# A planned attention and mixture-of-experts kernel: turns for VectorE and GpSimd, due times by product, another product order at group ends, an earlier warm-up

## The chip, the cores and the metric

The kernel runs on one core of a Trainium2 chip. The metric is device time in microseconds (us) of one execution. A kernel's time is the median of its runs; the profile shows one execution with its own time. TensorE multiplies matrices and does the transposes, VectorE and GpSimd do element-wise work, ScalarE does exponentials, casts and copies, and SyncE issues the DMA loads and stores. A profile calls them PE (PEld is its weight load), DVE, POOL, ACT and SP.

## The reference

Windowed attention feeds a dense mixture of four experts.

```python
scores = scale * np.matmul(q, k.transpose(0, 1, 3, 2))      # q, k, v: (4, 8, 576, 64)
rel = pos[:, None] - pos[None, :]
mask = (rel >= 0) & (rel < 64)
scores = np.where(mask, scores, -1e9)
attn = np.exp(scores - np.max(scores, axis=-1, keepdims=True))
attn = attn / (np.sum(attn, axis=-1, keepdims=True) + 1e-09)
x = np.matmul(attn, v).transpose(0, 2, 1, 3).reshape(2304, 512)
p = domain_probs / (domain_probs.sum(-1, keepdims=True) + 1e-09)
for e in range(4):
    h = np.maximum(x @ w1[e], 0.0)                           # w1[e]: (512, 1024)
    out += p[:, e:e + 1] * (h @ w2[e])                       # w2[e]: (1024, 512)
```

## The kernel before, in words

**The work.** The 2304 rows of x are three groups of 768. A group is made by 12 attention steps of 64 rows, numbered g = 0 to 35. Step g has scores on TensorE (`S`, tile `sb`), row maxima on VectorE (`st`), exponentials on ScalarE (`sm`), reciprocals on VectorE, the normalisation on GpSimd (`sm` again, line 356), a transpose on TensorE (`tb`), its copy (`pt`), the product with v on TensorE (`vb`) and a copy into the group's x^T tile `xr`.

For each group the four experts are 16 units of 256 hidden columns, 48 units in all. The units are numbered 0 to 47; units 16 and 32 are the first of the second and third group, units 15 and 31 the last before. Each matrix is split into a high part (a cast to fp32r) and a low part (the value minus the high part), and a product is three fp32r multiplications: high by high, high by low, low by high.

**First layer.** Units 0 and 1 multiply directly (tile `d`). All others use Strassen's scheme in Winograd's form: seven products P1 to P7 instead of eight, of the four quarters of x^T (B11, B12, B21, B22) and combinations of them (T1 to T4, made in `xr` itself by three-operand subtractions, line 426), with combinations of the raw weights `w1r` (sums on GpSimd, lines 468 to 471). A product is six matmuls of 384 columns. P1 goes to the PSUM bank X, P5 to V, P6 to Y; P7 and P4 add to Y, P2 adds to X, P3 to V. ScalarE copies P1's result to `s1`, and P2 may write X only after that. VectorE forms `u2`, `u3`, `c22`, `c21`, `c12` from the banks (line 595). The relu is split in turn: high part on ScalarE (line 535), low part on VectorE (line 538), both into tiles `h`.

**Second layer.** For a pair of units and each of six row tiles, two half steps of six matmuls (tile `y`, 128x512) multiply `h` with `w2s`. VectorE adds each finished `y`, scaled by p, to the accumulator `acc` (line 676). The low part of `w2s` is made on GpSimd (line 510), two instructions of 512 columns.

**The order.** The list `seq` fixes TensorE's order of products and second-layer halves. Everything else is a `Step` with a cost for each engine that may do it, a due time, the steps it comes after and the buffers it needs. `Planner.order` walks a clock for each engine, takes the ready step that can start first (among equals the one due first), puts it on the engine where it ends first and frees buffers. The steps are then emitted in the planned order, so each engine runs a fixed queue. A unit's halves of the second layer stand between the products of the next units, one after each product from the second on.

The loads stand in SyncE's one queue. Weights are reloaded for each group. `w1r` has two buffers, `w2r` one, `w2s` three, and each split piece of a unit's w1 (`w1a` to `w1d`) one.

**At a group's end.** The last unit of a group still needs the old x^T parts, so the splits of the next group's parts become possible one by one while the last unit's products run. The due times of all of them were counted from one number, `due0`, eight places ahead of the new group's first product.

**At the start.** 20 fp32 matmuls of 128 columns on the identity matrix (`warm`, line 716, 40 instructions) precede the first scores. The weights p are normalised by `prep` (lines 520 to 523, four VectorE instructions).

Of the kernel before, what the change touches and what calls it, by code (L numbers as in the profile page):

```python
# [29 lines left out]
class Step:  # L30
    def __init__(self, plan, name, engines, emit, due, after=(), takes=(), uses=(), seq=None):
        self.name, self.engines, self.emit, self.due, self.seq = name, engines, emit, due, seq
# [11 lines left out]
class Planner:  # L44
# [5 lines left out]
    def order(self):  # L50
# [3 lines left out]
        dma_free = 0.0  # L54
# [12 lines left out]
        while left:  # L67
            best = None
            for e, now in clock.items():
                cands = []  # L70
                for s in ready[e]:
                    if s.seq is not None and s.seq != seq_at:
                        continue
                    t = max(now, s.ready)
# [23 lines left out]
            clock[e] = end  # L98
            if e == "SP":
# [23 lines left out]
def kernel(ctx: ExitStack, tc: tile.TileContext, q, k, v, dprobs, w1, w2, out):  # L123
    nc = tc.nc
# [75 lines left out]
    def dvec(n):  # L200
        return 0.1 + 0.00056 * n

    def pool_(n):
        return 0.1 + 0.00225 * n

    def add(name, engines, emit, due, after=(), takes=(), uses=(), seq=None):
        return Step(plan, name, engines, emit, due, after, takes, uses, seq)
# [8 lines left out]
    FIRST = ("P1", "P2", "P5", "P6", "P7", "P4", "P3")  # L216
# [9 lines left out]
    for i in range(DIRECT, nun + 4):  # L226
# [5 lines left out]
        prods = [("p", i, j) for j in (FIRST if i % NU == 0 or i == DIRECT else ORDER)] if i < nun else []  # L232
# [20 lines left out]
    for g in range(NG):  # L253
# [97 lines left out]
        r = add(f"r{g}", dict(DVE=0.42), recip, due + 1.8, [e], [], [st])  # L351
# [6 lines left out]
        nm = add(f"n{g}", dict(POOL=0.05 + 0.00203 * NP * nk), norm, due + 2, [r], [], [sm, st])  # L358
# [39 lines left out]
    for n in range(NGRP):  # L398
        due0 = at["p", n * NU, "P1"] - 8 if n else at["p", DIRECT, "P1"] - 10
# [6 lines left out]
        def split(name, q_, after, due, n=n, quarter=quarter, src=src):  # L406
            b = comb[n, name] = Buf("T4" if name == "B12" else name)

# [9 lines left out]
            h = add(f"{name}h{n}", dict(ACT=act(KH * T), DVE=dvec(KH * T)), hi, due, after, [b], [src])  # L418
            l = add(f"{name}l{n}", dict(DVE=dve(KH * T), POOL=pool_(KH * T)), lo, due + 0.1, [h], [], [src, b])
# [3 lines left out]
        def diff(name, dst, a, b_, after, due, n=n, quarter=quarter, src=src):  # L423
# [4 lines left out]
            s = add(f"{name}d{n}", dict(DVE=dve(KH * T), POOL=pool_(KH * T)), sub, due, after, [], [src])  # L428
# [3 lines left out]
        b11 = split("B11", 0, x0, due0 if n else -60)  # L432
# [346 lines left out]
```

## Time and profile before

| | us |
|---|---|
| median of 3 runs | 868.26 |
| lowest and highest run | 867.0, 871.38 |
| the profiled execution's own time | 868.09 |
| its span, first to last instruction | 866.3 |
| TensorE busy in the span | 845.9 |
| VectorE busy | 605.0 |
| ScalarE busy | 358.0 |
| GpSimd busy | 330.6 |

TensorE is busy in 98% of the span, VectorE in 70%. The ends of matmuls are modelled in a profile, so durations of neighbours overlap; what a step costs TensorE is read from start to start. Outside the span lie 1.8 us.

### The profile page before, as it was taken

The page shows a single profiled execution, that of the slowest core. Times are in us where ns is not written, and L with a number is a line of the kernel's source. Part 1 is how long each engine was busy: PE and PEld are TensorE (multiplying, and loading weights), DVE is VectorE, ACT ScalarE, POOL GpSimd, SP SyncE. Part 2 cuts the span into 40 slices and gives each one's busy share as a digit, 9 for nine tenths or more (in the row PEclk, how much of TensorE's full clock was granted, in tenths as well). Part 3 has the DMA queues.
Part 4 walks back from the last instruction along what each step waited for, and adds up shares of the span by engine and source line. Part 5 has one row for each costly group of instructions (what it writes and reads, how often), then busy time and mean ns, then how long its engine had stood idle before and what let it go on. Part 6 is the DMA issues. An engine that isn't in the chain of part 4 may idle for free.

```text
span 866.3 us, 12968 instructions
## 1 busy us (share of the span) xinstructions
PE 845.9 (98%) x4816; PEld 755.0 (87%) x4816; DVE 605.0 (70%) x965; ACT 358.0 (41%) x825; POOL 330.6 (38%) x336
## 2 busy tenths in 40 slices
PE   7899999999999989999999999997999999999998
PEld 7788988888888888888888888886988988999896
DVE  3878767667676897666766767697667667667652
ACT  4645434445444455333443544343334334334320
POOL 3464424344244453342434424354243244333301
PEclk9999999999999999999999999998999999999999
DMA  9933313233233142312323212112232112212001
GB/s 308 301 111 104 97 50 97 96 101 104 92 113 114 49 153 98 122 61 74 119 78 120 72 39 84 63 48 86 75 108 73 57 66 73 74 49 97 26 24 73
DMA packets 45327, 81.23 MB, mean 94 GB/s; under 512 B 6352, under 2 KB 15568, under 8 KB 45264
## 3 DMA queue, kind: packets, MB, share of 16 engines
q1 hardware_dynamic: 45264, 80.40, 27.9%
q8 instruction: 38, 0.62, 0.3%
q14 instruction: 25, 0.20, 0.1%
HBM read 75.67 MB, written 4.72 MB: 93 GB/s over the span
## 4 chain that ended last, share of the span: by engine, by line
PE 90%; DVE 6%; DMA 2%; issue 1%; SPq 0%; ACT 0%; ACTq 0%
PE y L657 44%; PE Y L576 16%; PE X L576 11%; PE V L576 11%; PE sb L298 2%; PE vb L378 2%; PE tb L363 1%; PE d L629 1%; DVE T L416 1%; DVE xr L426 1%; DVE B L416 1%; DMA kt<-in_k_dram 1%; DMA vn<-in_v_dram 1%; DMA w1r<-in_moe_w_dram 1%; DVE h L538 0%
## 5 line engine op out<-in xcount | busy, mean ns | idle before, releaser
L657 PE MATMUL y<-w2s,h 128*128 128x512 f32 x1728 | 447.7, 396 | 0.0
L657 PEld LDWEIGHTS y<-w2s,h 128*128 128x128 f32 x1728 | 320.0, 188 | 52.1
L510 POOL TENSOR_TENSOR w2s<-w2r,w2s 128x512 fp32r<-128x512 f32 x96 | 135.8, 1436 | 164.2 <-ACT w2s L506 159.5
L676 DVE SCALAR_TENSOR_TENSOR acc<-y,dp,acc 128x512 f32<-128x512 f32 x126 | 94.1, 747 | 114.7 <-PE y L657 114.5
L468 POOL TENSOR_TENSOR w1r<-w1r 128x256 f32<-128x256 f32 x46 | 36.8, 801 | 229.6 <-DMA w1r<-in_moe_w_dram 206.9
L538 DVE SCALAR_TENSOR_TENSOR h<-c,h 128x384 fp32r<-128x384 f32 x138 | 112.6, 816 | 6.6 <-ACT h L535 6.5
L535 ACT ACTIVATE h<-c 128x384 fp32r<-128x384 f32 x138 | 72.4, 525 | 49.3 <-DVE c L595 45.9
L595 DVE TENSOR_TENSOR u<-Y,s 128x384 f32<-128x384 f32 x92 | 51.1, 555 | 48.6 <-PE Y L576 48.1
L506 ACT CAST w2s<-w2r 128x1024 fp32r<-128x1024 f32 x48 | 50.4, 1050 | 78.1 <-DMA w2r<-in_moe_w_dram 63.7
L356 POOL TENSOR_TENSOR sm<-sm,st 128x512 f32<-128x512 f32 (+1 forms) x36 | 38.8, 1078 | 111.0 <-DVE st L349 102.2
L486 ACT CAST w1b<-w1r 128x512 fp32r<-128x512 f32 x46 | 28.5, 619 | 98.0 <-PE Y L576 96.1
L595 DVE TENSOR_TENSOR c<-V,u 128x384 f32<-128x384 f32 x92 | 51.1, 556 | 24.2 <-PE V L576 22.7
L576 PE MATMUL X<-B,w1c 128*128 128x384 f32 x276 | 58.1, 346 | 7.1 <-ACT s L598 7.1
L576 PEld LDWEIGHTS X<-B,w1c 128*128 128x128 f32 x276 | 50.0, 191 | 11.2 <-ACT s L598 7.6
L486 ACT CAST w1c<-w1r 128x512 fp32r<-128x512 f32 x48 | 29.8, 620 | 64.9 <-PE Y L576 48.4
L576 PE MATMUL X<-B,w1a 128*128 128x384 f32 x276 | 56.5, 339 | 0.0
L576 PE MATMUL Y<-T,w1b 128*128 128x384 f32 x276 | 56.5, 339 | 0.0
L576 PE MATMUL V<-T,w1b 128*128 128x384 f32 x276 | 56.4, 339 | 0.0
L576 PE MATMUL Y<-T,w1a 128*128 128x384 f32 x276 | 56.3, 338 | 0.0
L576 PE MATMUL V<-B,w1d 128*128 128x384 f32 x276 | 56.2, 338 | 0.0
L576 PE MATMUL Y<-T,w1c 128*128 128x384 f32 x276 | 56.0, 337 | 0.0
L576 PEld LDWEIGHTS V<-T,w1b 128*128 128x128 f32 x276 | 50.3, 191 | 4.2
(77 smaller groups left out, 1128.3 us busy)
## 6 DMA issues: line engine op xcount, KB each, us to landing
w1r<-in_moe_w_dram SPq DMA_DIRECT2D x96, 256.0 KB, 3.1
w2r<-in_moe_w_dram SPq DMA_DIRECT2D x48, 512.0 KB, 3.6
qb<-in_q_dram SPq DMA_DIRECT2D x36, 256.0 KB, 4.5
vn<-in_v_dram SPq DMA_DIRECT2D x32, 256.0 KB, 4.4
kt<-in_k_dram SPq DMA_DIRECT2D x17, 384.0 KB, 4.0
out_dram<-acc SPq DMA_DIRECT2D x18, 256.0 KB, 2.0
vn<-in_v_dram SPq DMA_DIRECT2D x4, 128.0 KB, 3.5
kt<-in_k_dram SPq DMA_DIRECT2D x1, 256.0 KB, 4.1
```

The lines of the kernel that those rows point to most:

```text
L298: nc.tensor.matmul(t[:, p, :nk], qb.tile[:, p, :], kt[u].tile[:, p, end - nk : end], start=not pe_mask, stop=p == NP - 1 or not pe_mask,)
L356: nc.gpsimd.tensor_tensor(out=t, in0=t, in1=rl.to_broadcast([P, NP, nk]), op=ALU.mult)
L468: e.tensor_tensor(out=t[:, 2], in0=t[:, 1], in1=t[:, 5], op=ALU.add)
L486: f(t[:, 0], raw.tile[:, lo_:hi_])
L506: nc.scalar.copy(make(b, f"w2s{i}")[:, 0], raw.tile)
L510: nc.gpsimd.tensor_tensor(out=b.tile[:, 1, f], in0=raw.tile[:, f], in1=b.tile[:, 0, f].bitcast(F32), op=ALU.subtract)
L535: nc.scalar.activation(make(b, f"h{i}_{f}{t_}")[:, 0], src.tile[:, :T], AF.Relu)
L538: nc.vector.scalar_tensor_tensor(out=b.tile[:, 1], in0=src.tile[:, :T], scalar=0.0, in1=b.tile[:, 0].bitcast(F32), op0=ALU.max, op1=ALU.su ...
L576: nc.tensor.matmul(t[:, :T], wb.tile[:, a, wi, ws], cb.tile[:, x, c, :], start=first and m == 0, stop=m == 5, skip_group_check=True,)
L595: return lambda t, p_: nc.vector.tensor_tensor(out=t, in0=p_, in1=o.tile, op=ALU.add)
L657: nc.tensor.matmul(o, hh[:, a, ts], w[:, b, f, :], start=x == 0 and m == 0, stop=x == 1 and m == 5)
L676: nc.vector.scalar_tensor_tensor(out=ab.tile, in0=yb.tile, scalar=pc, in1=ab.tile, op0=ALU.mult, op1=ALU.add)
```

## The change

Seven edits.

1. A step has a list `port` of engines on which it reads two operands from SBUF (VectorE) or runs at all (GpSimd). The planner keeps one `port_free` time; such steps take turns in the plan. Steps of VectorE that read PSUM don't carry it. The costs of some steps are adjusted.
2. The splits and differences of x^T get a due time each, seven places ahead of the product that uses them.
3. The order `FIRST` changes to P1, P5, P2, ..., and the last unit of each group uses it too.
4. The four sums of a unit's raw weights become four steps, and each split piece waits only for the last sum that it reads. The two low halves of w2 become two steps.
5. `prep` comes after the splits of B11 and B21 of the first group.
6. The warm-up reads a zeroed bf16 tile instead of the identity, has 32 matmuls of 128 columns, and stands first in the program.
7. An exponential on a small tile, first on ScalarE, makes it load its function table at the start.

```diff
@@ Planner.order
-                    t = max(now, s.ready)
+                    t = max(now, s.ready, port_free if e in s.port else 0.0)
...
-                t2 = max(clock[e2], s.ready, t if clock[e2] <= t else clock[e2])
+                t2 = max(t, clock[e2], port_free if e2 in s.port else 0.0)
...
             clock[e] = end
+            if e in s.port:
+                port_free = end
@@ order of products
-    FIRST = ("P1", "P2", "P5", "P6", "P7", "P4", "P3")
+    FIRST = ("P1", "P5", "P2", "P6", "P7", "P4", "P3")
...
-        prods = [("p", i, j) for j in (FIRST if i % NU == 0 or i == DIRECT else ORDER)] if i < nun else []
+        prods = [("p", i, j) for j in (FIRST if i % NU in (0, NU - 1) or i == DIRECT else ORDER)] if i < nun else []
@@ x^T
-        due0 = at["p", n * NU, "P1"] - 8 if n else at["p", DIRECT, "P1"] - 10
+        first = n * NU if n else DIRECT
+        need = {PROD[x][1]: at["p", first, x] - 7 for x in PROD}
...
-            h = add(f"{name}h{n}", dict(ACT=act(KH * T), DVE=dvec(KH * T)), hi, due, after, [b], [src])
-            l = add(f"{name}l{n}", dict(DVE=dve(KH * T), POOL=pool_(KH * T)), lo, due + 0.1, [h], [], [src, b])
+            h = add(f"{name}h{n}", dict(ACT=act(KH * T), DVE=dvec(KH * T)), hi, due, after, [b], [src], port=("DVE",))
+            l = add(f"{name}l{n}", dict(DVE=dve(KH * T), POOL=pool_(KH * T)), lo, due + 0.1, [h], [], [src, b], port=("DVE", "POOL"))
@@ sums of the raw w1
+    COMBS = ((2, 1, 5, ALU.add), (3, 0, 1, ALU.subtract), (1, 2, 0, ALU.subtract), (6, 4, 1, ALU.subtract))
...
-            c = add(f"w1c{i}", dict(POOL=4 * (0.15 + 0.0024 * A)), comb_w1, due - 4, [ld], [], [raw])
+            step = add(f"w1s{i}_{dst}", dict(POOL=0.75), comb_w1, due - 4, [step], [], [raw], port=("POOL",))
+            made[dst] = step
...
-            h = add(f"{kind}h{i}", dict(ACT=act(m)), hi, due + lo_, [c], [b], [raw])
-            l = add(f"{kind}l{i}", dict(DVE=dve(m) + 0.15), lo, due + lo_ + 0.2, [h], [], [raw, b])
+            h = add(f"{kind}h{i}", dict(ACT=act(m)), hi, due + lo_, [made.get(hi_ - 1, ld)], [b], [raw])
+            l = add(f"{kind}l{i}", dict(DVE=dve(m)), lo, due + lo_ + 0.2, [h], [], [raw, b], port=("DVE",))
@@ prep
-    probs = add("prep", dict(DVE=1.3), prep, 5, [ldp])
+    probs = add("prep", dict(DVE=1.3), prep, 5, [ldp, *x_split])
@@ start of the program
+    warm = pool.tile([P, 2 * W], BF16, tag="s1_0", name="warm")
+    nc.vector.memset(warm, 0.0)
+    nc.vector.memset(dps, 0.0)
+    nc.scalar.activation(dps, dps, AF.Exp)
+    warm_out = psum.tile([P, DM], F32, tag="b2", name="warm_out")
+    for _ in range(WARM):
+        nc.tensor.matmul(warm_out[:, : 2 * W], warm, warm, start=True, stop=True)
...
-    warm = psum.tile([P, DM], F32, tag="b2", name="warm")
-    for _ in range(WARM):
-        nc.tensor.matmul(warm[:, :P], ident, ident, start=True, stop=True)
...
-WARM = 20
+WARM = 32
```

**TensorE at the second group end.** These are the instructions around the first products of unit 32 on TensorE's queue, before the change. A name like X32 is bank X of unit 32, y15 the second layer of the pair of units 30 and 31.

```order
L657 MATMUL y14_5_5818<-w2s29_5552,h29_11_5513 128x512 x3
L576 MATMUL X32_5855<-B11_2_5729,w1a_32_5739 128x384 x6
L576 MATMUL X32_5855<-B21_2_5804,w1c_32_5826 128x384 x6
L657 MATMUL y15_0_5883<-w2s30_5629,h30_00_5662 128x512 x3
L657 MATMUL y15_0_5883<-w2s30_5629,h30_10_5685 128x512 x3
L576 MATMUL V32_5898<-T1_2_5762,w1b_32_5779 128x384 x6
```

And the same place after the change:

```order
L663 MATMUL y14_5_5828<-w2s29_5568,h29_11_5529 128x512 x3
L582 MATMUL X32_5864<-B11_2_5745,w1a_32_5791 128x384 x6
L582 MATMUL V32_5879<-T1_2_5762,w1b_32_5813 128x384 x6
L663 MATMUL y15_0_5890<-w2s30_5651,h30_00_5675 128x512 x3
L663 MATMUL y15_0_5890<-w2s30_5651,h30_10_5702 128x512 x3
L582 MATMUL X32_5864<-B21_2_5772,w1c_32_5838 128x384 x6
```

P2, the second product into bank X, stood directly behind P1. Now P5 and a half of the second layer stand between them.

**VectorE at the second group end.** This is VectorE's queue ahead of unit 32 before the change (xr is a difference of x^T quarters; c21 and c12 of unit 31 free its banks Y and V).

```order
L538 SCALAR_TENSOR_TENSOR h31_00_5807<-X31_5708,h31_00_5807 128x384
L426 TENSOR_TENSOR xr2_3537<-xr2_3537 128x2x384
L490 TENSOR_TENSOR w1b_32_5779<-w1r32_5577,w1b_32_5779 128x512
L411 CAST T4_2_5845<-xr2_3537 128x768
L676 SCALAR_TENSOR_TENSOR acc1_4_3852<-y14_4_5772,dp_67,acc1_4_3852 128x512
L416 TENSOR_TENSOR T4_2_5845<-xr2_3537,T4_2_5845 128x768
L595 TENSOR_TENSOR c21_31_5862<-Y31_5720,s1_31_5727 128x384
L416 TENSOR_TENSOR B22_2_5847<-xr2_3537,B22_2_5847 128x768
L490 TENSOR_TENSOR w1c_32_5826<-w1r32_5577,w1c_32_5826 128x512
L595 TENSOR_TENSOR c12_31_5872<-V31_5743,u2_31_5741 128x384
L538 SCALAR_TENSOR_TENSOR h31_10_5867<-c21_31_5862,h31_10_5867 128x384
```

After the change:

```order
L420 TENSOR_TENSOR T2_2_5797<-xr2_3567,T2_2_5797 128x768
L601 TENSOR_TENSOR c22_31_5826<-V31_5736,u3_31_5815 128x384
L420 TENSOR_TENSOR T3_2_5817<-xr2_3567,T3_2_5817 128x768
L494 TENSOR_TENSOR w1b_32_5813<-w1r32_5594,w1b_32_5813 128x512
L682 SCALAR_TENSOR_TENSOR acc1_4_3886<-y14_4_5784,dp_67,acc1_4_3886 128x512
L430 TENSOR_TENSOR xr2_3567<-xr2_3567 128x2x384
L601 TENSOR_TENSOR c21_31_5861<-Y31_5775,s1_31_5743 128x384
L601 TENSOR_TENSOR c12_31_5873<-V31_5736,u2_31_5795 128x384
L682 SCALAR_TENSOR_TENSOR acc1_5_3944<-y14_5_5828,dp_67,acc1_5_3944 128x512
L544 SCALAR_TENSOR_TENSOR h31_11_5836<-c22_31_5826,h31_11_5836 128x384
L494 TENSOR_TENSOR w1c_32_5838<-w1r32_5594,w1c_32_5838 128x512
L544 SCALAR_TENSOR_TENSOR h31_10_5877<-c21_31_5861,h31_10_5877 128x384
```

The low parts of T4 and B22 moved behind c21 and c12. T2's low part and one difference, which were GpSimd's, are on VectorE now: at each group end all eleven two-operand steps on x^T are.

**VectorE ahead of the first product.** Before the change, from the copy of the sixth attention step's result (xr<-vb5) to the split of the first two quarters (dps and dp are `prep`):

```order
L388 COPY xr0_249<-vb5_424 128x4x64
L520 TENSOR_REDUCE dps_68<-dp_67 128x18
L521 TENSOR_SCALAR dps_68<-dps_68 128x18
L522 RECIPROCAL dps_68<-dps_68 128x18
L523 TENSOR_TENSOR dp_67<-dp_67,dps_68 128x72
L411 CAST B11_0_467<-xr0_249 128x768
L411 CAST B21_0_477<-xr0_249 128x768
```

After it:

```order
L390 COPY xr0_265<-vb5_446 128x4x64
L415 CAST B11_0_456<-xr0_265 128x768
L415 CAST B21_0_458<-xr0_265 128x768
L420 TENSOR_TENSOR B11_0_456<-xr0_265,B11_0_456 128x768
L420 TENSOR_TENSOR B21_0_458<-xr0_265,B21_0_458 128x768
L350 TENSOR_SCALAR st6_432<-st6_432 128x4
```

The four instructions of `prep` moved behind the splits.

## Rows read from the trace of the kernel before

**Rows 1.** Stages: length, busy PE, PEld, DVE, ACT, POOL, clock, DMA share, GB/s.

```profile
0.00:92.00 92.00, 82.49 (x665) 74.28 (x666) 66.56 (x136) 49.41 (x176) 39.80 (x50) 1.00 0.61 200
92.00:290.00 198.00, 198.00 (x1163) 176.41 (x1162) 137.84 (x221) 86.13 (x196) 78.82 (x80) 1.00 0.29 94
290.00:320.00 30.00, 27.80 (x150) 24.95 (x149) 28.25 (x37) 14.05 (x29) 15.10 (x10) 1.00 0.28 93
320.00:570.00 250.00, 250.00 (x1441) 222.74 (x1440) 175.68 (x284) 107.94 (x252) 98.16 (x100) 1.00 0.26 87
570.00:605.00 35.00, 30.09 (x136) 26.69 (x135) 28.55 (x37) 13.28 (x22) 17.08 (x14) 0.90 0.20 66
```

**Rows 2.** Timeline, second group end: start, duration, engine, instruction, [idle before, releaser].

```profile
585.87 3.23 POOL L510 TENSOR_TENSOR w2s<-w2r,w2s 128x512 fp32r<-128x512 f32 x2 [0.69 <-ACT w2s L506]
586.38 1.59 DVE L426 TENSOR_TENSOR xr<-xr 128x768 f32<-128x768 f32 x1
...
587.90 1.75 DVE L490 TENSOR_TENSOR w1b<-w1r,w1b 128x512 fp32r<-128x512 f32 x1
...
593.09 2.29 PE L576 MATMUL X<-B,w1c 128*128 128x384 f32 x6 [4.91 <-ACT s L598]
...
599.44 1.54 PE L657 MATMUL y<-w2s,h 128*128 128x512 f32 x6
```

**Rows 3.** Timeline of TensorE behind the first group end's wait.

```profile
314.86 1.55 PE L657 MATMUL y<-w2s,h 128*128 128x512 f32 x6
...
316.25 1.21 PE L576 MATMUL V<-T,w1b 128*128 128x384 f32 x6
...
317.29 1.55 PE L657 MATMUL y<-w2s,h 128*128 128x512 f32 x6
```

**Rows 4.** Timeline of VectorE at the first group end, GpSimd idle.

```profile
293.00 0.56 DVE L411 CAST B<-xr 128x768 fp32r<-128x768 f32 x1
...
293.60 0.96 DVE L416 TENSOR_TENSOR B<-xr,B 128x768 fp32r<-128x768 f32 x1
...
294.94 0.95 DVE L426 TENSOR_TENSOR xr<-xr 128x768 f32<-128x768 f32 x1
...
295.81 0.68 DVE L490 TENSOR_TENSOR w1a<-w1r,w1a 128x512 fp32r<-128x512 f32 x1
```

**Rows 5.** Groups by line: busy us, mean ns of one, idle us before.

```profile
L676 DVE SCALAR_TENSOR_TENSOR acc<-y,dp,acc 128x512 f32<-128x512 f32 x126 | 94.1, 747 | 114.7 <-PE y L657 114.5
```

**Rows 6.** Timeline of the start, all engines.

```profile
1.18 0.65 SPq L276 DMA_DIRECT2D kt<-in_k_dram  x1
...
1.36 6.58 PE L716 MATMUL warm<-ident 128*128 128x128 f32 x40 [1.36 <-POOL ident masks.py:199]
...
4.12 0.56 SPq L278 DMA_DIRECT2D kt<-in_k_dram  x1
...
9.64 1.28 ACT L319 ACT_TABLE_LOAD   x1 [9.64 <-DVE st L312]
...
9.83 0.38 PE L296 MATMUL sb<-maskb,identb 128*128 128x512 bf16 x1
...
10.05 1.06 PE L298 MATMUL sb<-kt,qb 128*128 128x128 f32 x8
...
13.49 0.63 PE L363 MATMUL tb<-ident,sm 128*64 128x128 f32 x4 [2.38 <-POOL sm L356]
```

**Rows 7.** DMA of the first 30 us: engine, count, KB each, median us to landing.

```profile
kt<-in_k_dram SPq DMA_DIRECT2D x5, 384.0 KB, 5.8
...
kt<-in_k_dram SPq DMA_DIRECT2D x1, 256.0 KB, 4.1
```

**Rows 8.** Timeline of VectorE ahead of the first direct product.

```profile
30.49 0.21 DVE L520 TENSOR_REDUCE dps<-dp 128x18 f32<-128x72 f32 x1
...
32.68 1.02 DVE L411 CAST B<-xr 128x768 fp32r<-128x768 f32 x2
```

**Rows 9.** Timeline of TensorE, direct products.

```profile
34.62 1.14 PE L629 MATMUL d<-B,w1a 128*128 128x384 f32 x5 [0.89 <-DVE B L416]
...
69.78 1.34 PE L629 MATMUL d<-B,w1a 128*128 128x384 f32 x6 [1.45 <-DVE h L538]
```

**Rows 10.** Warm-up matmuls alone, two stretches: TensorE busy (matmuls), weight loads, granted clock.

```profile
3.30:4.30 1.00, 1.00 (x7) 1.00 (x7) 1.00 1.05 264
5.30:6.30 1.00, 1.00 (x11) 1.00 (x10) 1.00 0.81 297
```

More of the change, by code (lines that the diff above doesn't have):

```diff
@@ L30, with __init__ @@
 class Step:
-    def __init__(self, plan, name, engines, emit, due, after=(), takes=(), uses=(), seq=None):
-        self.name, self.engines, self.emit, self.due, self.seq = name, engines, emit, due, seq
+    def __init__(self, plan, name, engines, emit, due, after=(), takes=(), uses=(), seq=None, port=()):
+        self.name, self.engines, self.emit, self.due, self.seq, self.port = name, engines, emit, due, seq, port
         self.after, self.takes, self.uses = [a for a in after if a is not None], list(takes), list(uses)
@@ L203, in pool_, with add @@
     def pool_(n):
-        return 0.1 + 0.00225 * n
-    def add(name, engines, emit, due, after=(), takes=(), uses=(), seq=None):
-        return Step(plan, name, engines, emit, due, after, takes, uses, seq)
+        return 0.1 + 0.00215 * n
+    def add(name, engines, emit, due, after=(), takes=(), uses=(), seq=None, port=()):
+        return Step(plan, name, engines, emit, due, after, takes, uses, seq, port)
     def dma(nbytes):
@@ L349, in recip @@
             nc.vector.reciprocal(t[:, 3], t[:, 3])
-        r = add(f"r{g}", dict(DVE=0.42), recip, due + 1.8, [e], [], [st])
+        r = add(f"r{g}", dict(DVE=0.42), recip, due + 1.8, [e], [], [st], port=("DVE",))
         def norm(on, nk=nk, st=st, sm=sm):
@@ L404, in quarter, with split @@
             return xr[n].tile[:, d * KH : (d + 1) * KH, t * T : (t + 1) * T]
-        def split(name, q_, after, due, n=n, quarter=quarter, src=src):
+        def split(name, q_, after, due=None, n=n, quarter=quarter, src=src):
             b = comb[n, name] = Buf("T4" if name == "B12" else name)
+            due = need[name] if due is None else due
             def hi(on):
@@ L506, in hi2, with lo2 @@
             nc.scalar.copy(make(b, f"w2s{i}")[:, 0], raw.tile)
-        def lo2(on, b=b2, raw=raw2):
-            for f in range(2):
+        h = add(f"w2h{i}", dict(ACT=act(2 * DM)), hi2, due, [ld], [b2], [raw2])
+        w2p[i], w2_done[i] = b2, [h]
+        for f in range(2):
+            def lo2(on, b=b2, raw=raw2, f=f):
                 nc.gpsimd.tensor_tensor(
@@ L512, in lo2 @@
                 )
-        h = add(f"w2h{i}", dict(ACT=act(2 * DM)), hi2, due, [ld], [b2], [raw2])
-        l = add(f"w2l{i}", dict(POOL=pool_(2 * DM)), lo2, due + 0.2, [h], [], [raw2, b2])
-        w2p[i], w2_done[i] = b2, [h, l]
+            w2_done[i].append(
+                add(f"w2l{i}{f}", dict(POOL=1.25), lo2, due + 0.2, [h], [], [raw2, b2], port=("POOL",))
+            )
     def prep(on):
@@ L525, with hidden @@
     ldp = add("ldp", dict(SP=1.0), lambda on: nc.sync.dma_start(dp, dprobs.rearrange("(n p) e -> p n e", p=P)), -20)
-    probs = add("prep", dict(DVE=1.3), prep, 5, [ldp])
+    probs = add("prep", dict(DVE=1.3), prep, 5, [ldp, *x_split])
     bank, hb, h_done, evac = {}, {}, {}, {}
     ybank, ystep, accb, acc_step = {}, {}, {}, {}
-    def hidden(i, f, t_, src, after, due):
+    def hidden(i, f, t_, src, after, due, port=()):
         b = hb[i, f, t_] = Buf(f"h{t_}")
@@ L610 @@
                 c21 = tmp("c21", addto(s1), pb, [s, evac[i, "s1"]], [s1])
-                hidden(i, 1, 0, c21, [evac[i, "c21"]], due + 3)
+                hidden(i, 1, 0, c21, [evac[i, "c21"]], due + 3, ("DVE",))
             elif pname == "P3":
                 c12 = tmp("c12", addto(u2), pb, [s, evac[i, "u2"]], [u2])
-                hidden(i, 0, 1, c12, [evac[i, "c12"]], due + 3)
+                hidden(i, 0, 1, c12, [evac[i, "c12"]], due + 3, ("DVE",))
         elif key[0] == "d":
```

58 lines of the change are left out of this document (28 added, 30 removed).

## The prediction

> **What bounds the kernel now.** I read the busy time by stage first. In the long stretches inside the groups TensorE is busy 198.00 of 198.00 and 250.00 of 250.00 us at the full clock [rows 1]; there nothing that another engine does can bring time, only cost it. TensorE stands still in three places: the first 92 us (82.5 busy), the first group end (27.8 of 30.0) and the second (30.1 of 35.0, clock 0.90 on the mean) [rows 1]. So the question is what the change does there, and whether it opens a wait in a full stretch.
>
> At the second group end the timeline shows TensorE 4.91 us idle ahead of P2 of unit 32, released by ScalarE's copy `s1` [rows 2]. ScalarE was not slow: the copy stands in its queue behind the relu of `c21`, and `c21` stands in VectorE's queue behind x^T work. Behind the wait the clock is at the lower of its two levels (1.2 GHz): from 593.09 to 599.44 one product, one half of the second layer and one product take 6.35 us [rows 2]. At full clock a half takes 1.39 us from start to start and a product 1.04 [rows 3], so these three are worth 3.47, and the clock cost 2.88. The first end has the same wait, with three scores steps in TensorE's queue inside it, and lost 30.0 - 27.8 = 2.2 us at full clock [rows 1].
>
> VectorE and GpSimd get in each other's way. Alone, a 768-column difference takes 0.95 us and a 512-column low part 0.68 [rows 4]; beside GpSimd's low part of w2 they took 1.59 and 1.75 [rows 2], so 0.6 to 1.1 more.
>
> **The start, in three terms.** (a) The first scores need k's first load, which lands at 1.18 + 4.1 = 5.3 us [rows 6, 7], but the warm-up holds TensorE to 1.36 + 6.58 = 7.9. The exponential then waits for a table load of 1.28 us [rows 6]. The first transpose starts at 13.49 after 2.38 idle [rows 6]. Both causes go, 2.6 + 1.3 = 3.9 us, but not all of it arrives. In the queue that transpose stands behind the third scores, which need the second load of k: 4.12 + 5.8 = 9.9 us [rows 6, 7], just when they start now (9.83 with the mask, [rows 6]); the order of the loads there does not change. Those scores end at 10.05 + 1.06 = 11.1 [rows 6], so the transpose can come 2.4 us earlier. Its own chain allows that: from the end of the warm-up to the transpose are 5.6 us now, 4.3 without the table load, which from 5.3 gives 9.6. I take 2.4 and let the following steps keep their pace; 0 if later loads hold them, 3.9 if no load does.
>
> (b) `prep` stands between the sixth attention step's copy and the split of B11, and takes 32.68 - 30.49 = 2.2 us there [rows 8]. It moves behind the splits. What needs it is the first accumulation of the second layer, more than 10 us later. The direct products wait for that split (0.89 us at 34.62, [rows 9]), so all 2.2 count, and they start 4.6 earlier.
>
> (c) Later one direct product waits 1.45 us for a relu's low part on VectorE, which frees its PSUM bank [rows 9]. VectorE was late there with x^T work beside GpSimd. In the new order GpSimd's next long step behind two normalisations, the low part of unit 2's w2, waits for a cast that ScalarE has only behind this stage, so I take the wait as gone: 1.4, from 0 to 1.45.
>
> Sum 2.4 + 2.2 + 1.4 = 6.0, bounds 2.2 and 7.5.
>
> **The second group end.** Count from the start of P1 of unit 31. TensorE then has its seven products, P1 of unit 32 and six halves ahead of P5 of unit 32, which needs bank V, freed by `c12` of unit 31: 8 x 1.04 + 6 x 1.39 = 16.7 us [rows 3]. In the new queue VectorE has from the last relu part of unit 30 up to that `c12`: nine differences and low parts of 768 columns, from start to start 0.87 (294.94 to 295.81); three casts of 0.56; two 512-column low parts of 0.68; one relu part and five additions of (294.94 - 293.60) - 0.87 = 0.47 [rows 4]; three accumulations of 0.75 [rows 5]. That is 7.8 + 1.7 + 1.4 + 2.8 + 2.25 = 15.95. So VectorE arrives just in time, with 0.7 us to spare. P2 comes 2.43 us behind P5 now, with one product and one half between, and `c21` stands ahead of `c12`, so `s1` is no longer the last to come. P2 also needs w1c's low part, three instructions behind `c12`, 0.75 + 0.47 + 0.68 = 1.9 us: again just in time.
>
> This holds if GpSimd does not interfere. Its low part of w2 of unit 31 can begin when the half that reads the old buffer is through, about 14 us into the count, so it meets the last difference and the three SBUF steps behind `c12`. At 0.6 to 1.1 each that is up to 4.4 us of delay; the plan's turns and 0.7 of slack work against it. Of 0 to 3.5 us of wait I take 0.9, one collision. Waits of 2.38 us at the start and about 2.2 at the first end left the clock at 1.00 [rows 1, 6], so a wait of 0.9 should not cost the clock. Gain: 4.91 + 2.88 - 0.9 = 6.9, bounds 4.3 and 7.8.
>
> The Trainium skill (SBUF — State Buffer, Who interferes with whom) calls the shared port an exclusive lock that the loser waits for through a whole instruction. It speaks against the turns, since a plan cannot set who comes first on the chip; by it each of the four steps could lose a whole GpSimd instruction, and this end would gain only the lower bound. Beside it, [rows 2] shows losses up to about that size.
>
> **The first group end.** The same, with two scores steps of about 1 us ahead in TensorE's queue as extra slack. I leave 0.4 of the 2.2: gain 1.8, bounds 0.9 and 2.2.
>
> **Nothing for the rest.** In the full stretches the same instructions run, and TensorE's ones hide them [rows 1]. Split sums and changed costs alter places only. If that cover is gone they cost 0 to 4 us; I take 0.
>
> **Sum.** 6.0 + 6.9 + 1.8 = 14.7 us from the profiled execution's 868.1 (866.3 of span and 1.8 around it), which is 0.2 below the median of the runs: 853.4.
>
> **The rivals.**
>
> VectorE becomes the bound of the group ends. It takes two x^T steps more from GpSimd at each, and the count above has 0.7 us of slack. With every collision a full one the second end waits 3.5, the first gains nothing, and the wait may again pull the clock down (2.88). Then 868.1 - 6.0 - 4.3 = 857.8, or 860.7 with the clock. For it speaks that VectorE is busy 28.25 of 30.0 us at the first end [rows 1]; against it that GpSimd is free in most of the count.
>
> The clock is low at the start. In the old warm-up 7 matmuls fall into 3.3 to 4.3 us and 11 into 5.3 to 6.3 [rows 10]: the clock rose in between, though the column reads 1.00. A bf16 mask product of 512 columns takes 10.05 - 9.83 = 0.22 us [rows 6], so 32 of 128 columns take 32 x 0.11 = 3.5 at the lower level. The new warm-up is over at about 4.6, near that rise, and TensorE then idles until 5.3. If the clock isn't up, the third scores end 1.1 later, and more steps may be slow: 1.1 to 4 us lost, 854.5 to 857.4. The Trainium skill (TensorE: Matmul & The Clock Gate, What's actually happening) says that the throttled state is the default and that activity releases it. By that rule a shorter warm-up is a risk, and the sum would be this rival's; the trace shows the rise but not which amount it needs.
>
> Loads hold the start, so that of it only `prep` counts: 868.1 - 2.2 - 8.7 = 857.2. For it speaks a DMA share of 0.61 over the first stage [rows 1]; against it that it moves the same bytes in the same order.
>
> Slower: the new GpSimd queue makes the full stretches wait. TensorE's queue is fixed, and each of the 24 transposes of groups two and three waits for a normalisation on GpSimd that now stands among single sums, some behind a load. To lose 0.5% (4.3 us) net these must wait 14.7 + 4.3 = 19 us, 0.8 each; at 1.0 each, 868.1 - 14.7 + 24 = 877. It decides from 0.8. Against it: now not one of them waits in 448 us [rows 1], and the normalisations stand between complete sets of sums except at group ends.
>
> The change does nothing: the waits only move to the next low part and the start is bound by loads: 866 to 868.
>
> **How the numbers follow.** Forecast (850 to 857) 0.56, VectorE bound 0.16, clock low 0.12, loads 0.08, slower 0.05, nothing 0.03. About 0.5% is what a measurement of this kernel tells from no change, so faster means below 863.9. All cases but the last two lie there, less 0.04 for a rival's tail: 0.88 faster, 0.07 same, 0.05 slower. The upper bounds of the gains, all together, give 868.1 - 17.5 = 850.6; the range starts at 850 and goes to 862, over the rivals' prices, which leaves out less than 2 in 10.
>
> **What would show it.** Right: the table load ends before 5 us and the first scores start near 5.3; the first transpose near 11; the B11 split right behind the copy, the first direct products near 30; no wait above 1 us ahead of unit 16's and 32's P2, and clock 1.00 at the second end. Wrong: scores of twice the duration in the first 10 us; VectorE's steps stretched beside w2's low part and TensorE waiting ahead of P5 or P2 of unit 32; idle ahead of transposes inside a group, released by GpSimd.

## The result and the profile after

| | before | after |
|---|---|---|
| median of 5 runs, us | 867.9 | 853.83 |
| lowest and highest run | 867.0, 871.38 | 853.81, 853.9 |
| span of the profiled execution | 866.3 | 852.0 |
| TensorE, VectorE, GpSimd busy | 845.9, 605.0, 330.6 | 841.6, 585.6, 309.8 |

The ratio is 0.9832, 95% interval 0.9812 to 0.9851: 14.1 us less, where 14.7 were forecast (853.4). That the sum came out so close is partly luck: of its three places the start was forecast 1.2 us too large and the first group end 0.9 too small, and the runs before the change spread by 4.4 us. The busy times by stage answer to [rows 1]. The stretches are set earlier, so that each again holds the start, the long middles and the two group ends; columns as there.

```profile
0.00:87.00 87.00, 81.36 (x685) 72.26 (x686) 64.69 (x137) 49.97 (x183) 35.34 (x48) 1.00 0.65 214
87.00:285.00 198.00, 198.00 (x1135) 176.87 (x1133) 134.20 (x221) 86.36 (x194) 78.31 (x80) 1.00 0.28 93
285.00:315.00 30.00, 30.00 (x165) 27.39 (x165) 27.71 (x42) 13.74 (x28) 8.42 (x9) 1.00 0.32 102
315.00:562.00 247.00, 247.00 (x1422) 220.00 (x1422) 169.81 (x285) 106.89 (x249) 96.11 (x100) 1.00 0.26 87
562.00:598.00 36.00, 34.98 (x175) 31.15 (x175) 32.36 (x48) 14.85 (x26) 12.35 (x12) 1.00 0.17 59
```

The full stretches stayed full. At the first group end TensorE now has no idle time at all, at the second 1.02 us, and the clock stays at 1.00 there (0.90 before).

To see where the time came from I compare when TensorE starts P1 of one and the same unit. At units 10, 24 and 40 it has done the same work in both kernels, so the difference is the time saved up to there. One execution stands on each side. From unit 10 on, eight profiles of the changed kernel's order (the changed kernel itself and experiments 1, 2 and 4 to 8) agree within 0.2 us; up to unit 10 they differ by 2.3, so the first row carries that much of chance.

| P1 of unit | before | after | saved up to here | saved since the row above |
|---|---|---|---|---|
| 10 | 203.80 | 198.96 | 4.84 | 4.84 (start) |
| 24 | 450.56 | 443.01 | 7.55 | 2.71 (first group end) |
| 40 | 720.40 | 706.16 | 14.24 | 6.69 (second group end) |

**The start.** Rows from the timeline of the start after, all engines; they answer to [rows 6].

```profile
0.73 1.28 ACT L699 ACT_TABLE_LOAD   x1 [0.73 <-PEq L771]
...
0.99 3.59 PE L702 MATMUL warm_out<-warm 128*128 128x128 bf16 x32 [0.99 <-DVE dps L698]
...
5.24 1.94 PE L300 MATMUL sb<-kt,qb 128*128 128x64 f32 x8 [0.45 <-DMA kt<-in_k_dram]
...
7.40 2.06 PE L300 MATMUL sb<-kt,qb 128*128 128x128 f32 x8
...
10.23 1.13 PE L300 MATMUL sb<-kt,qb 128*128 128x128 f32 x8 [0.35 <-DMA kt<-in_k_dram]
...
11.52 0.63 PE L365 MATMUL tb<-ident,sm 128*64 128x128 f32 x4 [0.15 <-POOL sm L358]
```

The table load is out of the way, and the first scores start when k's first load lands, at 5.24. But they take 1.94 us and the second 2.06, where scores of the second's shape took 1.06 at full clock [rows 6]: behind the short warm-up TensorE works at the pace of the lower level (1.2 GHz). The clock column reads 1.00 there, but the trace's first clock record of this execution is at 9.9 us; ahead of it only the durations tell the clock. The third scores wait for k's second load all the same, and the first transpose starts at 11.52 instead of 13.49.

**The second group end.** Rows of VectorE and TensorE at P7 of unit 31 after:

```profile
571.80 0.95 DVE L430 TENSOR_TENSOR xr<-xr 128x768 f32<-128x768 f32 x1
...
572.67 0.55 DVE L601 TENSOR_TENSOR u<-Y,s 128x384 f32<-128x384 f32 x1
...
573.27 1.32 PE L582 MATMUL Y<-T,w1b 128*128 128x384 f32 x6 [1.02 <-DVE u L601]
```

P7 adds to bank Y, which `u2` must have read. `u2` stands behind T2's difference in VectorE's queue. This 1.02 us is TensorE's only listed wait from 92 us to the end, where 7.1 us in two waits stood before. VectorE and GpSimd lose less to each other, too. Take instructions of one operation and one shape as a kind, and count those that took at least 0.15 us more than the lower quartile of their kind: VectorE's excess is 85.1 us in 114 instructions before and 57.4 in 95 after, and each of them overlaps a GpSimd instruction.

### The profile page after: what moved, and what is told of

It reads as the page before. It is cut to its first block, busy times and chain, and to the rows that moved or that the text cites. A ratio compares the mean times of both kernels' runs of the same rounds, so it can differ in the third digit from the quotient of the medians.

```text
span 852.0 us, 12957 instructions
## 1 busy us (share of the span) xinstructions
PE 841.6 (99%) x4808; PEld 751.0 (88%) x4808; DVE 585.6 (69%) x974; ACT 356.7 (42%) x825; POOL 309.8 (36%) x330
## 4 chain that ended last, share of the span: by engine, by line
PE 96%; DVE 2%; DMA 0%; issue 0%; POOL 0%; ACT 0%; SPq 0%; POOLq 0%; DVEq 0%
PE y L663 47%; PE Y L582 17%; PE X L582 11%; PE V L582 11%; PE sb L300 4%; PE vb L380 2%; PE tb L365 2%; PE d L635 1%; DMA kt<-in_k_dram 0%; DVE st L313 0%; DVE B L420 0%; PE sb L298 0%; POOL sm L358 0%; DVE B L415 0%; DVE acc L682 0%
## 5 line engine op out<-in xcount | busy, mean ns | idle before, releaser
L477 POOL TENSOR_TENSOR w1r<-w1r 128x256 f32<-128x256 f32 x184 | 141.9, 782 | 218.1 <-DMA w1r<-in_moe_w_dram 203.5
L516 POOL TENSOR_TENSOR w2s<-w2r,w2s 128x512 fp32r<-128x512 f32 x96 | 128.2, 1356 | 201.3 <-ACT w2s L510 200.8
L544 DVE SCALAR_TENSOR_TENSOR h<-c,h 128x384 fp32r<-128x384 f32 x138 | 102.2, 741 | 11.2 <-ACT h L541 10.9
L582 PEld LDWEIGHTS Y<-T,w1b 128*128 128x128 f32 x276 | 49.1, 188 | 5.2 <-DVE u L601 1.6
L582 PEld LDWEIGHTS X<-B,w1a 128*128 128x128 f32 x276 | 49.2, 188 | 4.3 <-ACT h L541 0.7
```

The lines of the kernel that those rows point to most:

```text
L477: nc.gpsimd.tensor_tensor(out=t[:, dst], in0=t[:, x], in1=t[:, y], op=op)
L516: nc.gpsimd.tensor_tensor(out=b.tile[:, 1, f], in0=raw.tile[:, f], in1=b.tile[:, 0, f].bitcast(F32), op=ALU.subtract)
L544: nc.vector.scalar_tensor_tensor(out=b.tile[:, 1], in0=src.tile[:, :T], scalar=0.0, in1=b.tile[:, 0].bitcast(F32), op0=ALU.max, op1=ALU.su ...
L582: nc.tensor.matmul(t[:, :T], wb.tile[:, a, wi, ws], cb.tile[:, x, c, :], start=first and m == 0, stop=m == 5, skip_group_check=True,)
```

## The experiments

Experiments 1, 2, 3, 8 and 12 move single steps in the planned order, so that every other instruction keeps its place. The planner's list is changed once it is made:

```diff
     steps = plan.order()
+    by = {s.name: s for s in steps}
+    def move(name, ahead_of):
+        steps.remove(by[name])
+        steps.insert(steps.index(by[ahead_of]), by[name])
```

Runs of one and the same kernel differ by 2 us and more here, so a difference of about 1 us between two medians whose runs overlap shows little by itself. Each experiment is therefore also read by its profiled execution: by how much earlier (+) or later (-) than in the changed kernel P1 of units 10, 24 and 40 starts.

| run | median (lowest to highest) | unit 10 | unit 24 | unit 40 |
|---|---|---|---|---|
| prep at its old place | 853.58 (853.14 to 854.44) | -0.11 | -0.12 | -0.14 |
| prep late | 853.42 (853.23 to 853.98) | +0.03 | -0.15 | -0.16 |
| u2 first | 853.67 (853.25 to 855.79) | -2.21 | -2.22 | -1.96 |
| no early table load | 854.79 (853.59 to 855.8) | -0.92 | -0.90 | -0.93 |
| the changed kernel again | 854.01 (853.37 to 855.37) | -0.06 | -0.06 | -0.09 |
| old warm-up | 854.98 (854.35 to 855.54) | -1.67 | -1.67 | -1.71 |
| longer warm-up | 854.93 (853.66 to 856.13) | -2.26 | -2.26 | -2.28 |
| k's second load earlier | 855.15 (854.75 to 856.34) | -1.01 | -1.01 | -1.02 |
| no turns | 877.95 (876.41 to 881.14) | -7.95 | -13.63 | -22.58 |
| old order of products | 859.78 (857.3 to 861.33) | +0.19 | -1.46 | -3.91 |
| one due time | 857.05 (856.46 to 857.55) | +0.99 | -0.08 | -2.64 |
| late probabilities | 852.78 (852.46 to 854.12) | +0.91 | +0.91 | +1.19 |

**1. prep at its old place.**

```diff
+    move("prep", "B11h0")
```

> The changed kernel with one move: prep stands where it stood before, between the copy of the sixth attention step and the split of B11; every other instruction keeps its place. The step of the prediction (all 2.2 us of prep count): 853.8 + 2.2 = 856.0. Rival, prep's time is given back: in the changed kernel it takes 1.9 us at 33.8 instead, ahead of a copy that TensorE then waits 0.86 us for; the first direct product then comes 1.9 us later, and the stretch behind it 1 to 2 us faster: 853.8 to 854.6.

853.58 us: the rival holds. Rows of VectorE and TensorE of this run:

```profile
27.52 0.22 DVE L526 TENSOR_REDUCE dps<-dp 128x18 f32<-128x72 f32 x1
...
28.44 1.02 DVE L415 CAST B<-xr 128x768 fp32r<-128x768 f32 x2
...
29.80 1.10 PE L300 MATMUL sb<-kt,qb 128*128 128x64 f32 x8 [1.34 <-DMA qb<-in_q_dram]
30.71 1.29 PE L635 MATMUL d<-B,w1a 128*128 128x384 f32 x6
...
70.64 1.28 PE L582 MATMUL X<-B,w1a 128*128 128x384 f32 x6 [0.52 <-DVE h L544]
```

And the same places after the change:

```profile
29.24 1.31 PE L635 MATMUL d<-B,w1a 128*128 128x384 f32 x6
...
34.06 1.10 DVE L527 TENSOR_SCALAR dps<-dps 128x18 f32<-128x18 f32 x1
...
37.18 0.69 PE L380 MATMUL vb<-pt,vn 128*64 128x64 f32 x16 [0.86 <-DVE pt L371]
...
70.52 1.30 PE L582 MATMUL X<-B,w1a 128*128 128x384 f32 x6 [0.52 <-DVE h L544]
```

The first direct product comes 1.47 us later in this run, but it waits for no split: the scores ahead of it wait 1.34 us for a load of q. At its old place `prep` takes 0.92 us (27.52 to 28.44), with GpSimd idle. Before the change it took 2.2 [rows 8], beside GpSimd's low part of w2, whose rows read:

```profile
30.17 2.49 POOL L510 TENSOR_TENSOR w2s<-w2r,w2s 128x512 fp32r<-128x512 f32 x2
...
30.73 0.74 DVE L521 TENSOR_SCALAR dps<-dps 128x18 f32<-128x18 f32 x1
...
31.81 0.94 DVE L523 TENSOR_TENSOR dp<-dp,dps 128x72 f32<-128x72 f32 x1
```

In this experiment the same two steps take 0.18 and 0.23. At its new place `prep` meets GpSimd's low part of w2 again: one of its 18-column steps takes 1.10 us, and the attention copy behind it keeps TensorE waiting 0.86. So unit 2 starts only 0.12 us later with `prep` at its old place, and both kernels wait the same 0.52 us there for the same relu part on VectorE. What `prep` alone would do to the first direct product isn't shown, since the load held this run there.

**2. prep late.**

```diff
+    move("prep", "d0_0")
```

> The changed kernel with one move: prep stands directly ahead of the first accumulation of the second layer, about 27 us later than now. Theory, prep gave back most of its gain at 33.8 us: 0.9 to 1.7 us faster, 852.1 to 852.9. Rival, the start is held by other steps (loads, the chain of normalisations): 853.8 within 0.3. Third, the first accumulation then comes too late for the second layer's bank: slower, up to 855.

853.42 us, unit 10 at +0.03: the rival. The 0.86 us wait is gone, and the wait ahead of unit 2 is 0.76 instead of 0.52. All three places of `prep` lie ahead of unit 2 in VectorE's queue, and which of them it has makes no difference to the total that these runs could show.

**3. u2 first.**

```diff
+    move("u2_31", "T2d2")
```

> The changed kernel with one move at the second group end: u2 of unit 31 stands ahead of the difference T2 on VectorE. Theory, the 1.02 us that TensorE waits ahead of P7 of unit 31 is this one place in VectorE's queue: 1.0 us faster, 852.8. Rival, VectorE as a whole is the bound of the group end, so the wait turns up again at P2 or P6 of unit 32: 853.8 within 0.3.

Its profiled execution lost 2.2 us in the start, 500 us ahead of the edit. From unit 24 to unit 40 it gained 2.22 - 1.96 = 0.26 of the 1.02 us. The wait ahead of P7 shrinks to this, from the timeline of TensorE:

```profile
574.62 1.33 PE L582 MATMUL Y<-T,w1b 128*128 128x384 f32 x6 [0.16 <-DVE u L601]
```

The rest turns up ahead of P7 and P4 of unit 31 and P7 of unit 32: from the start of the half before each to its own start are 0.15 to 0.31 us more than the 1.39 of a half. So the rival is nearer: VectorE is just full at this group end (in this run 36.48 of 40.0 us from 560 to 600, and all 15.0 from 575 to 590), and the place of one step brings a quarter of the wait. The median, 853.67, lies within the spread of the changed kernel's runs.

**4. No early table load.**

```diff
-    nc.vector.memset(dps, 0.0)
-    nc.scalar.activation(dps, dps, AF.Exp)
```

> The changed kernel without the early exponential: the function table is loaded ahead of the first exponential of the scores again. The 1.28 us of the load carried through: 855.1. Rival, it was hidden already by the third scores, which wait for k's second load (they end at 11.3, and the transpose stands behind them), and by the row maximum of the second step in VectorE's queue: 0 to 0.3 us, 853.8 to 854.1.

854.79 us: by the median 0.8 more than the changed kernel in the next experiment, on another chip and with runs that overlap. Its profile shows something neither expectation names. Timeline rows, and a window with the granted clock (third column from the end):

```profile
6.85 1.28 ACT L321 ACT_TABLE_LOAD   x1 [6.85 <-DVE st L314]
...
10.37 1.75 PE L300 MATMUL sb<-kt,qb 128*128 128x128 f32 x8 [2.47 <-DMA kt<-in_k_dram]
...
11.92 1.06 PE L365 MATMUL tb<-ident,sm 128*64 128x128 f32 x4
```

```profile
12.00:16.00 4.00, 4.00 (x36) 3.52 (x35) 2.35 (x8) 2.23 (x10) 1.04 (x1) 0.74 1.07 401
```

The table load lies inside the wait for k's second load, as the rival said. But here the first two scores ran at full clock, so TensorE waited 2.47 us, and the clock fell: the third scores take 1.75, the transpose 1.06 (0.63 after the change). Whether the table load or this accident makes the 0.8 us isn't settled by these runs.

**5. The changed kernel again**, unaltered.

> The changed kernel itself, unaltered, on this chip, as the measure for the others: 853.8. If the start is decided by when k's second load lands and by where TensorE's clock stands then, its runs spread over 1 to 2.5 us (the spans of earlier profiles differ by up to 2 us, all of it in the first 14 us); if not, they agree within 0.1 us.

Five runs from 853.37 to 855.37 us on this chip; the five of the result lay within 0.1. The spread is that of the first expectation. That it lies in the start is taken from the other profiles, which agree from unit 10 on; only one of these five executions was profiled.

**6. The old warm-up**, 20 fp32 matmuls on the identity, behind the masks.

> The changed kernel with the old warm-up in its old place (20 fp32 matmuls on the identity, behind the masks), the early table load kept. The step of the prediction (the shorter warm-up is worth 2.4 us less the table load): the first scores start at 7.9 again, the first transpose near 12.2 instead of 11.5: 0.7 us slower, 854.5. Rival, the clock: the long warm-up keeps the clock up until the third scores, which wait for k's second load in any case: no loss, 853.2 to 853.8, and less spread between runs.

854.98 us, 1.0 more than experiment 5 on the same chip, with runs that overlap. The first transpose, from the timeline:

```profile
12.06 0.63 PE L365 MATMUL tb<-ident,sm 128*64 128x128 f32 x4 [0.52 <-POOL sm L358]
```

It is 0.8 us later than in experiment 5 (11.27), as the first expectation has it (0.7). With the old warm-up the early table load alone moves it from 13.49 [rows 6] to 12.06, 1.43 us. The spread of the runs is smaller (1.2 us against 2.0), but the clock still fell once, to 0.75 between 20 and 24 us.

**7. A longer warm-up.**

```diff
-WARM = 32
+WARM = 48
```

> The changed kernel with 48 warm-up matmuls instead of 32, so that they last until about 5.3 us, when k's first load lands. Theory, the short warm-up leaves the clock low for some of the first scores (1.94 us instead of 1.0): they run at full clock, but the third scores still wait for k's second load: 0 to 0.3 us faster, 853.5 to 853.8. Rival, the clock is what holds the start: 1 us faster, 852.8. Third, the wait for the load is longer by what the scores are faster, and the clock falls in it: up to 1 us slower, 854.8.

854.93 us, spread over 2.5 us. In the profile the first transpose, at 10.97, is earlier than in any experiment before it, and still the execution is 2.26 us late at unit 10. TensorE's timeline shows the place, and a window behind it the granted clock:

```profile
27.95 2.08 PE L300 MATMUL sb<-kt,qb 128*128 128x128 f32 x8 [1.40 <-DMA qb<-in_q_dram]
```

```profile
28.00:32.00 4.00, 4.00 (x18) 3.94 (x19) 3.48 (x8) 1.23 (x3) 1.97 (x2) 0.50 0.96 317
```

A wait of 1.40 us for a load of q, behind several shorter ones, and the clock is at 0.50 for the next four. So the third expectation is right in its kind (a wait in which the clock falls), at another load than it named. In these four runs a longer warm-up doesn't steady the start.

**8. k's second load earlier.**

```diff
+    move("lk1", "lv0")
```

> The changed kernel with one load moved: k's second load is issued directly behind the first, ahead of two loads of v and two of q. Theory, the third scores wait for that load (0.35 to 2.5 us idle ahead of them): the load lands 1 us or more earlier, the first transpose starts at 10.4 to 10.9 instead of 11.5, 0.6 to 1.1 us faster, 852.7 to 853.2. Rival, the loads share the same engines, so the second and third scores now wait for q instead, or the steps behind keep their pace: 853.8 within 0.3.

855.15 us, 1.1 more than experiment 5, with runs that overlap: the rival, and more. The second scores now wait for q, from the timeline:

```profile
8.41 2.08 PE L300 MATMUL sb<-kt,qb 128*128 128x128 f32 x8 [1.88 <-DMA qb<-in_q_dram]
```

With k's second load ahead of it, SyncE issues this load of q at 3.21 us; after the change it does so at 2.55, and the second scores start at 7.40 without a wait for it. What the move gained at one load it lost at another.

**9. No turns.**

```diff
-                    t = max(now, s.ready, port_free if e in s.port else 0.0)
+                    t = max(now, s.ready)
...
-                t2 = max(t, clock[e2], port_free if e2 in s.port else 0.0)
+                t2 = max(clock[e2], s.ready, t if clock[e2] <= t else clock[e2])
```

> The changed kernel with edit 1 undone in the planner: steps with two SBUF operands no longer take turns with GpSimd's; all else as changed. T2's difference and low part go back to GpSimd at each group end, and T4's low part and B22's stand ahead of c12 of unit 31 again. Theory, the turns are what shortened the group ends: VectorE's steps stretch by 0.6 to 1.1 us beside GpSimd's, c12 comes 2 to 5 us late for P5 of unit 32 and the clock falls there: 857 to 862. Rival, the product order alone did it: 853.8 to 855.3.

877.95 us, ratio to before 1.0098 (1.0077 to 1.0119): slower than the kernel before, with the other six edits and the changed costs of edit 1 in place, and far outside both expectations. It loses 8.0 us in the start, 5.7 at the first and 8.9 at the second group end. The second end, GpSimd, VectorE and TensorE from their timelines:

```profile
585.18 1.81 POOL L430 TENSOR_TENSOR xr<-xr 128x768 f32<-128x768 f32 x1 [0.89 <-DVE T L420]
...
585.49 2.32 DVE L420 TENSOR_TENSOR B<-xr,B 128x768 fp32r<-128x768 f32 x1
...
589.01 2.46 POOL L420 TENSOR_TENSOR T<-xr,T 128x768 fp32r<-128x768 f32 x1 [0.62 <-DVE T L415]
...
590.19 1.83 DVE L494 TENSOR_TENSOR w1a<-w1r,w1a 128x512 fp32r<-128x512 f32 x1
...
590.33 2.29 PE L582 MATMUL Y<-T,w1b 128*128 128x384 f32 x6 [4.44 <-DVE u L601]
...
604.24 1.28 PE L582 MATMUL V<-T,w1b 128*128 128x384 f32 x6 [2.88 <-DVE c L601]
```

With T2 on GpSimd again, B21's low part takes 2.32 us (0.96 alone) and w1a's 1.83 (0.68). `u2` is 4.44 us late, the clock falls (P7 takes 2.29), and `c12` makes a second wait of 2.88. In the start two direct products wait 3.95 and 1.97 us for steps of VectorE. VectorE's excess by the count above is 89.1 us in 126 instructions, about as before the change. The run undoes two things at once: steps collide again, and T2's difference and low part are back on GpSimd, where they take 1.81 and 2.46 us (0.95 each on VectorE after the change). How much each of them costs isn't separated.

**10. The old order of products.**

```diff
-    FIRST = ("P1", "P5", "P2", "P6", "P7", "P4", "P3")
+    FIRST = ("P1", "P2", "P5", "P6", "P7", "P4", "P3")
...
-        prods = [("p", i, j) for j in (FIRST if i % NU in (0, NU - 1) or i == DIRECT else ORDER)] if i < nun else []
+        prods = [("p", i, j) for j in (FIRST if i % NU == 0 or i == DIRECT else ORDER)] if i < nun else []
```

> The changed kernel with edit 3 undone: P2 stands directly behind P1 in the first unit of a group, and the last unit has the usual order. Theory, P5 and a half of the second layer between P1 and P2 are what took the wait ahead of P2 away (2.43 us of slack): it comes back at 2.4 us or more, and the clock falls behind it: 856.2 to 860. Rival, the turns and due times brought VectorE's queue forward, so s1 is early in either order: 853.8 to 854.8.

859.78 us: the theory by the time, though the wait ahead of P2 is shorter than its 2.4 us. TensorE's timeline at the second end of its fastest kind of run (857.73):

```profile
582.71 0.61 PE L582 MATMUL X<-B,w1c 128*128 128x384 f32 x2 [0.62 <-ACT s L604]
584.33 0.97 PE L582 MATMUL X<-B,w1c 128*128 128x384 f32 x4 [1.01 <-DVE w1c L494]
585.14 2.42 PE L663 MATMUL y<-w2s,h 128*128 128x512 f32 x6
```

P2 waits for `s1` and then for w1c's low part, 1.63 us in all, and the clock falls behind it: the half takes 2.42 us instead of 1.55. This end loses 3.91 - 1.46 = 2.45 us, the first 1.65. Three of the five runs stand at a lower clock over the whole span (0.993, against 0.997 and 0.998) and 2 to 4 us higher.

**11. One due time.**

```diff
-        need = {PROD[x][1]: at["p", first, x] - 7 for x in PROD}
+        due0 = at["p", first, "P1"] - (8 if n else 10)
+        need = dict(B11=due0, B21=due0 + 1, B22=due0 + 4, T1=due0 + 2.1, T2=due0 + 2.3, T3=due0 + 3.1, T4=due0 + 3.6)
```

> The changed kernel with edit 2 undone: the x^T steps get their due times from one number again. T4's difference and the cast of B22 then stand ahead of c21 and c12 of unit 31, and two steps of T4 and B22 ahead of w1c's low part. Theory, the due times by product matter: 1 to 3 us slower, 855 to 857, waits ahead of P5 and P2 of unit 32. Rival, VectorE has the same work in any order: 853.8 within 0.3.

857.05 us, 3 us slower: the theory, at its upper end. TensorE's list of waits in this run from 80 us on (us in total, times, longest):

```profile
PE V L583 <- ACT h L542: 1.5, 1, 1.5
PE X L583 <- DVE w1c L495: 1.4, 2, 0.8
PE Y L583 <- DVE u L602: 1.0, 1, 1.0
```

The first is P5 of unit 32, and P2 waits for w1c at both ends, the places expected. The group ends lose 1.07 and 2.56 us. In the start this execution is 0.99 us ahead at unit 10, and no run shows whether that is the order of the x^T steps or chance.

**12. Late probabilities.**

```diff
+    move("ldp", "lv13")
+    move("prep", "d0_0")
+    move("u2_31", "T2d2")
```

> The changed kernel with three moves: the load of the expert weights p goes 18 places back in SyncE's queue, prep directly ahead of the first accumulation, and u2 of unit 31 ahead of T2's difference. Theory, the 4.6 to 5.7 us that the issue of w2's first load takes behind the load of p hold q's load for the ninth scores (1.3 to 1.4 us of wait in two profiles, and a low clock behind one of them): 0.5 to 1.3 us faster than the changed kernel, 852.5 to 853.3, with less spread. Rival, VectorE's x^T work ahead of unit 2 holds the end of the start, so that only u2's 0.3 us is left: 853.5 to 853.8.

852.78 us, ratio to before 0.981 (0.9793 to 0.9828); faster than the kernel before, and by the median 1.05 less than the changed kernel's 853.83, whose runs in experiment 5 overlap with these. The issue of w2's first load in this run, and the q loads behind it, from SyncE's timeline:

```profile
16.95 0.53 SPq L505 DMA_DIRECT2D w2r<-in_moe_w_dram  x1
17.68 1.77 SPq L269 DMA_DIRECT2D qb<-in_q_dram  x2
```

After the change the same two places read:

```profile
17.73 5.65 SPq L505 DMA_DIRECT2D w2r<-in_moe_w_dram  x1
23.48 0.85 SPq L269 DMA_DIRECT2D qb<-in_q_dram  x2
```

The first of these q loads is issued 5.8 us earlier, and no scores between 11 and 40 us wait for a load. But none do in the changed kernel's own profile either, so this pair doesn't show the theory's cause. Of the gain 0.91 us lies ahead of unit 10: at the first transpose (10.93 against 11.52) this execution is ahead by 0.59 already, and the wait of 0.86 behind `prep` is gone. Another 0.28 lies at the second end, where `u2` stands as in experiment 3. The spread of the runs is 1.7 us, so the start isn't steady yet.

## Why the prediction was right, point by point

**The first term of the start, 2.4 us: right at its place.** The first transpose came 1.97 us earlier, and k's second load was what held it, as worked out: the third scores wait 0.35 to 2.47 us for it in the twelve profiles that keep its place. How much of this arrives at unit 10 isn't shown. In experiment 10 the first transpose was another 0.62 us earlier and unit 10 only 0.19, in experiment 7 it was 0.55 us earlier and unit 10 came 2.26 later.

**prep, 2.2 us: wrong.** It was counted whole because the direct products wait for the split behind it. They do come earlier, but experiments 1 and 2 put `prep` at three places and the total doesn't move by more than 0.2 us in the profiles. The step that failed is "so all 2.2 count", in two ways. The 2.2 us weren't `prep`'s own: with GpSimd idle it takes 0.92, and the rest was GpSimd's low part of w2 beside it, which it meets again at its new place. And the term ended at the first direct product and didn't ask what ends last in the stage. Ahead of unit 2, at 70 us, TensorE waits for VectorE, which is busy 9.53 and 9.46 of 10 us in the two stretches from 50 to 70 and has `prep` to do ahead of that at any of the three places.

**The wait of 1.45 us in the direct products, 1.4: the mechanism was right, the net size smaller.** The wait is gone, and GpSimd's low part of w2 comes only behind this stage, as worked out:

```profile
71.81 2.55 POOL L516 TENSOR_TENSOR w2s<-w2r,w2s 128x512 fp32r<-128x512 f32 x2 [15.01 <-ACT w2s L510]
```

But a wait of 0.52 us for another relu's low part now stands ahead of unit 2, so 0.9 are left of it. Of the start's 4.84 us, 1.97 came by the first transpose. In the other 2.9 the direct products' waits of 0.89 and 1.45 us [rows 9] are gone, and the new waits of 0.86 and 0.52 stand against them; which edit brought how much of it no run separates. With the turns undone the start loses 8.0 us, in waits of the same kind (3.95 ahead of a direct product, for a relu's low part). The whole start was forecast at 6.0 and gave 4.84.

**The second group end, 6.9 us: the size right, the place wrong.** It gave 6.69, and the wait left was 1.02 us where 0.9 were forecast, and the clock stayed at 1.00. But the forecast put it at P5 or P2 of unit 32, and it stands at P7 of unit 31. The count compared VectorE's whole queue with TensorE's between two end points, 15.95 against 16.7 us. That total was good, as experiment 3 shows (VectorE has hardly any slack), but it doesn't see a step in between that TensorE needs sooner, here `u2`.

**The first group end, 1.8 us: too small.** It gave 2.71, above the forecast's upper bound of 2.2, and no wait is left. The bound held the wait alone. Before the change P2 behind it also took 1.35 us from start to start (to 314.86, [rows 3]), where a product takes 1.04:

```profile
313.51 1.51 PE L576 MATMUL X<-B,w1c 128*128 128x384 f32 x6 [2.20 <-ACT s L598]
```

The two together are 2.5 us.

**The turns.** The forecast gave them no term of their own and took each of four steps to lose 0.6 to 1.1 us at worst. Experiment 9 shows that the other edits depend on them: without them the due times and the new order end 8 us above the kernel before, run beside it. In experiment 9 a step of 0.96 us took 2.32, beside a GpSimd instruction of 1.81 that started 0.31 us ahead of it. The Trainium skill (SBUF — State Buffer, Who interferes with whom) tells of an exclusive lock for which the loser waits through a whole instruction; this pair agrees with it. The doubt drawn from it, that a plan cannot set who comes first on the chip, held in part only: with the turns VectorE's excess fell from 85.1 to 57.4 us, and 57.4 are left.

**The rivals.** The clock was low at the start as the second rival said, 2.06 us for the second scores instead of 1.06, which the forecast had named as a sign of being wrong. The Trainium skill (TensorE: Matmul & The Clock Gate, What's actually happening), by which the throttled state is the default and activity releases it, is in line with these rows. The low clock cost nothing by itself in that execution, since the third scores wait for a load anyway. Loads hold part of the start, as the third rival said. VectorE is the bound of the second group end, but one wait of 1.02 us is all that it costs. The slower case did not come: no transpose inside a group waits for GpSimd, since the 1.02 us is the only wait listed from 92 us on.

What stays open: how much of the first term belongs to the table load with the new warm-up in place (0 to 0.8 us by experiment 4), how the start's gain divides among the edits, and why the changed kernel's runs agreed within 0.1 us on one chip and spread over 2 us on another.

## What to carry to other kernels

A stall that goes is worth what it moves at the end of its stage: name the instruction that ends last there before a term is counted whole. Where two queues are counted against each other, compare them at each step that one needs from the other, not at the two ends alone. Edits that order work around a shared resource don't add up: the same other edits that gain 14 us with the turns lose 8 without them.

## What the hardware showed that I had not expected

- In the first 30 us a wait of 1.4 to 2.5 us between scores is followed by the lower clock in several profiles (granted 0.50 in 28 to 32 us of experiment 7, 0.74 in 12 to 16 of experiment 4), but not in all: behind the 1.99 us that the third scores of experiment 12 wait, it stays at 1.00. Runs of one kernel spread by 2 us.
- Behind the load of p, whose elements are 16 bytes long, SyncE's issue of the next load took 4.57 to 6.11 us in all thirteen profiles that keep its place; with that load elsewhere the same issue took 0.53.
- Beside GpSimd's low part of w2 a VectorE step of 18 columns took 1.10 us; the same step took 0.18 in experiment 1 with GpSimd idle.
